# All fill-in places of the attention stage are numbered anew; the last step of a small transposed product stands further behind ScalarE's copy

## The chip, the core and the metric

The kernel runs on one core of a Trainium2 chip. A core has TensorE for matrix products and transposes (PE in the rows; its weight loads are PEld), VectorE (DVE), ScalarE (ACT), GpSimd (POOL), and SyncE (SP), whose queue issues most of the transfers. They read their instructions in program order and meet through semaphores. The metric is the time of one execution on the device, in microseconds (us).

## What the kernel computes

Three parts follow one another; `B, H, S, D = 4, 8, 768, 64`.

```
q_assign, k_assign = argmax of (normalised q, k) . (normalised centroids)      # 16 clusters per head
scores = scale * q @ k.T, and -1e9 where q_assign != k_assign
attn   = exp(scores - max(scores)) / (sum + 1e-9);   x = attn @ v              # x: 3072 x 512
h = x @ w_in;  g = h * cos(h);  y = g @ w_out                                   # 512 -> 2048 -> 512
logits = y @ phi;  dispatch = softmax over tokens;  combine = softmax over slots
out = combine @ (relu((dispatch.T @ y) @ w1) @ w2)                              # 8 experts, 4 slots each
```

## The kernel before

**The attention stage** covers the first half of the time and is the only part that the change touches. The 32 (batch, head) combinations are taken as 16 pairs of heads. For each pair `i` a *stack* `st` in on-chip memory (three of them, used in turn) holds q and k, each split in a high and a low part, and rows that carry the cluster mask and the row maximum. A score tile is the sum of two products with this stack (lines 446 and 447, `s<-st`), `score` has one tile of 128 keys by 384 queries for each head `h` and step `u` (12 steps a pair), and ScalarE turns each tile into exponentials (line 450, `a<-s`). So one pair is 12 steps of two score tiles, 48 products of line 446/447, and this loop over 16 x 12 steps `g` is written once:

```
for g in range(GE):
    for h in range(2):
        run_fill(g, h)
        score(i, ...)
    run_fill(g, 2); psum_add(i, u); run_fill(g, 3)
```

**Everything else of the stage is filled in between.** `run_fill(g, pos)` issues what has been put at position `pos` (0 to 3) of step `g`; positions 0 and 1 are ahead of the step's first and second score tile, 2 and 3 behind them. Tables of numbers set the places: a number `x` means step `g + x//4` from the pair's own start, position `x % 4`, and the fraction orders what shares a position. `FIRST` is for the first pair, `POS` for the 13 pairs in the middle, `NEXT` and `LAST` for the last two. What is placed:

- the next pair's stack: transposes of q and k (`T`: `prep_T`, `tpq`, `tpk`, line 268), the high and low parts (`prep_hi`, `prep_lo`), the cluster products, maxima and mask rows (`c`, `m`, `rows`), and copies within the stack, which are put off for some positions (`defer`) and then issued by SyncE (line 175)
- the row maxima: 24 products `sm` for each pair (line 400), each followed by a reduction on VectorE (line 402); `fin` gathers them, transposes them (`mrow`, line 415) and copies two rows into the stack through SyncE (`smax_row`)
- the value products `av` (line 459, `o<-a,vt`): 12 groups of 4; their order in the table decides how many stand side by side
- sums of the exponentials (`sumq`), sums of v (`prep_vm2`, `vm`)
- the conversion of 64-bit weights to 32 bits, two blocks a pair, in 8 steps `cv` on VectorE, ScalarE and GpSimd (`conv_do`), and the load `cl` of the next block
- for half of the blocks a small product with phi in three steps `wp`: four transposes `wt`, four products `wp` whose result ScalarE copies to `wq` (line 552), and a transpose of that, `wr` (line 556, `wphi_sum`), whose result VectorE sums

`prep_T` (from the third pair's stack on), `sm`, `mrow`, `cl`, `ct`, `eqt`, `mt`, `vm`, `sum`, `wt`, `wp` and `wr` share a ring of three banks of the product memory, taken in program order (`mbank`): a product waits until the bank of the third one before it has been read. Score tiles have three banks of their own, value products one.

In the first pair the mask rows of its own stack are written late: `rows0(1, 0, h, ACT)` (line 367), for the second half of the queries, whose places are `r0c`. The products `sm` of the first pair for queries of that half (`sm0`) and its later score tiles read them.

Of the kernel before, what the change touches and what calls it, by code (L numbers as in the profile page):

```python
# [26 lines left out]
def clustered_attention_then_soft_moe(  # L27
# [51 lines left out]
    vm = const.tile([P, NPAIR], F32, name="vm")  # L79
# [71 lines left out]
    with ExitStack() as a:  # L151
# [9 lines left out]
        T = {}  # L161
# [408 lines left out]
        def at4(g, q, f, *args):  # L570
# [1 line left out]
            at(g + x // 4, x % 4, f, *args, rank=q - x if q != x else 0.5)  # L572

        POS = {
            "T": [1.308, 13.876, 1.089, 5.872, 25.746, 36.055, 14.541, 35.775],
            "c": [16.843, 31.522],
            "m": [32.535, 32.994, 33.715, 36.49],
            "rows": [36.873, 43.945, 43.068, 42.752],
            "ld": 32.617,
            "cv": [[1.267, 6.08, 6.296, 16.916, 17.01, 17.372, 17.997, 18.854], [23.969, 30.541, 31.284, 32.698, 46.461, 46.996, 47.088, 47.142]],  # L580
            "wp": [22.636, 36.3, 36.578],
            "sm": [28.2, 31.753, 25.657, 7.038, 27.872, 18.018, 29.863, 4.585, 33.271, 20.202, 11.647, 6.495, 37.608, 42.706, 46.397, 45.847, 46.576, 24.17, 36.506, 9.889, 1.582, 37.875, 41.562, 38.508],
            "fin": [1.573, 5.263, 34.676, 37.539],
            "vm": [34.193, 45.742, 15.753],
            "cl": [2.501, 42.906],
            "av": [33.349, 33.353, 33.357, 33.361, 33.365, 33.369, 49.465, 49.469, 49.473, 49.477, 49.481, 49.485],
        }
        FIRST = {
            "T": [11.933, 13.351, 14.016, 14.265, 22.414, 33.022, 23.121, 40.828],
            "c": [20.876, 24.238],  # L590
            "m": [24.829, 25.602, 27.504, 31.599],
            "rows": [35.559, 41.933, 35.178, 47.346],
            "ld": 27.056,
            "hl1": [4.573, 11.085, 2.498, 12.153],
            "p1": [0.493, 6.362, 8.509, 9.612, 10.885, 13.533],
            "rows1": [20.017, 14.551, 20.333, 15.204],
            "one1": 12.589,
            "ld2": 3.852,
            "cl0": 22.601,
            "sm0": [0.73, 3.159, 0.429, 5.394, 1.277, 0.812, 14.931, 17.953, 16.508, 13.98, 15.389, 15.817, 16.123, 18.564, 11.559, 18.991, 9.813, 16.449],  # L600
            "fin0": [7.049, 9.9, 19.506, 19.912],
            "sm1": [33.923, 25.966, 23.596, 34.913, 28.869, 21.44, 22.363, 35.531, 30.988, 25.828, 21.408, 31.03, 31.941, 31.182, 37.18, 44.547, 46.392, 41.954, 41.697, 45.967, 47.974, 41.852, 45.504, 36.04],
            "fin1": [35.625, 40.713],
            "vm": [2.043, 5.623],
            "av": [15.327, 16.374, 19.171, 19.479, 22.394, 27.138, 31.368, 35.743, 35.838, 43.045, 46.406, 47.768],
            "r0c": [0.631, 0.302],
        }
        NEXT = {
            "cv": [[0.394, 0.437, 0.698, 2.152, 6.295, 7.495, 8.058, 19.811], [9.426, 12.828, 16.693, 17.691, 17.936, 20.568, 23.949, 35.345], [27.565, 29.065, 29.167, 30.486, 34.096, 36.446, 36.936, 41.49]],
            "wp": [19.895, 23.514, 35.069, 43.672, 45.817, 47.564],  # L610
            "sm": [21.695, 24.397, 11.934, 7.684, 27.445, 16.489, 17.35, 1.48, 1.969, 22.001, 24.625, 29.74, 13.73, 36.394, 19.994, 32.733, 41.217, 44.01, 39.92, 43.68, 45.934, 33.344, 5.07, 42.168],
            "fin": [0.258, 6.344, 30.741, 34.194],
            "vm": [6.804, 16.472, 23.722],
            "cl": [3.32, 18.679, 25.571],
            "av": [14.329, 14.502, 14.506, 14.551, 22.244, 22.964, 34.139, 34.149, 34.159, 43.43, 43.459, 57.281],
        }
        LAST = {
            "cv": [[1.943, 3.444, 3.447, 3.887, 3.892, 3.901, 4.34, 14.881], [11.025, 13.344, 14.301, 14.914, 17.834, 24.542, 29.982, 31.011], [33.835, 34.438, 38.539, 38.774, 42.047, 45.521, 46.04, 47.203]],
            "wp": [36.509, 39.65, 42.446],
            "fin": [1.822, 4.268],  # L620
            "vm": [5.423, 24.404, 26.852],
            "cl": [3.923, 23.538],
            "xp": [4.425, 5.64, 17.033],
            "av": [14.033, 14.043, 14.092, 14.388, 26.165, 26.175, 38.144, 38.279, 38.307, 38.559, 59.688, 61.83],
        }

        def place_conv(n, g, pl, x):
# [771 lines left out]
```

## Time and profile before

| | us |
|---|---|
| median of 3 runs | 879.15 |
| the runs | 878.90, 879.15, 2150.93 |
| the profiled execution | 879.05 |
| its span, first to last instruction | 877.2 |

| engine | busy us | share of the span | instructions |
|---|---|---|---|
| PE | 858.8 | 98% | 5978 |
| PEld | 617.9 | 70% | 5978 |
| DVE | 666.3 | 76% | 1391 |
| ACT | 628.4 | 72% | 1307 |
| POOL | 461.8 | 53% | 345 |

Busy time is the union of the instructions' spans on an engine; products overlap one another on PE, so its share says whether it had work, not how fast it went. The chain of work that ended last lies on PE for 93% of the span and on ACT for 3%. The attention stage ends at about 440 us; the MLP and the experts follow and use the engines in the same way before and after the change.

### The profile page before, as it was taken

To read this page: it belongs to the slowest core of one execution; us is meant where nothing else is said; L and a number is where in the kernel's file an instruction comes from. 1 tells how busy PE (TensorE), PEld (TensorE's weight loads), DVE (VectorE), ACT (ScalarE), POOL (GpSimd) and SP (SyncE) were. 2 spreads that over 40 slices of the span, in tenths; PEclk is the share of its full clock that TensorE was granted. 3 is DMA by queue.
4 is the path that set the end of the run, shared out by engine and by line. 5 is a ranking of instruction groups with operands and counts; after the bars stand their busy time and mean duration, and the time that the engine had idled before them with its cause. 6 is when DMAs were issued, how large, how long until landed. Compare 5 with 4: busy or idle time off the path is not lost.

```text
span 877.2 us, 16786 instructions
## 1 busy us (share of the span) xinstructions
PE 858.8 (98%) x5978; PEld 617.9 (70%) x5978; DVE 666.3 (76%) x1391; ACT 628.4 (72%) x1307; POOL 461.8 (53%) x345
## 2 busy tenths in 40 slices
PE   8999999999999999999999999999999999999995
PEld 4676767676777776776578877877787787777453
DVE  6798898988898988899877767776776777766203
ACT  6898888898888898886656775765666576577323
POOL 4578889888898888898953222222322222210000
PEclk9999999999999999999999999999999999999997
DMA  8766766656766656744323233321011010178998
GB/s 185 178 164 173 178 177 160 177 157 173 185 172 166 166 162 175 178 141 129 115 60 98 86 130 121 90 79 49 25 31 43 25 49 25 48 270 312 386 374 292
DMA packets 124742, 129.50 MB, mean 148 GB/s; under 512 B 57850, under 2 KB 101108, under 8 KB 124660
## 3 DMA queue, kind: packets, MB, share of 16 engines
q1 hardware_dynamic: 122948, 128.02, 50.2%
q8 instruction: 47, 0.77, 0.4%
q10 hardware_dynamic: 1712, 0.43, 0.3%
q14 instruction: 35, 0.29, 0.1%
HBM read 86.18 MB, written 16.97 MB: 118 GB/s over the span
## 4 chain that ended last, share of the span: by engine, by line
PE 93%; ACT 3%; DVE 1%; DMA 1%; issue 0%; ACTq 0%; DVEq 0%
PE h L139 30%; PE o L459 15%; PE sm L400 8%; PE s L446 8%; PE s L447 7%; PE gt L894 5%; PE lp L924 2%; PE accp L1007 2%; PE he L1240 2%; PE so L1269 2%; PE sum L484 1%; PE cl L308 1%; PE tpk L268 1%; PE tpq L268 1%; PE wt L542 1%; PE fo L1316 1%
## 5 line engine op out<-in xcount | busy, mean ns | idle before, releaser
L477 POOL TENSOR_TENSOR ps<-ps,a 128x768 f32<-128x768 f32 x124 | 229.9, 1854 | 37.5 <-ACT a L450 31.3
L139 PE MATMUL h<-wc,xhi 128*128 128x512 f32 x768 | 248.6, 404 | 0.0
L402 DVE TENSOR_REDUCE mc<-sm 128x1 f32<-128x384 f32 x384 | 195.9, 551 | 39.3 <-PE sm L400 38.3
L450 ACT ACTIVATE a<-s 128x384 f32<-128x384 f32 x384 | 174.0, 495 | 13.2 <-PE s L447 10.0
L139 PEld LDWEIGHTS h<-wc,xhi 128*128 128x128 f32 x768 | 137.1, 188 | 38.6 <-issue 11.7
L139 PE MATMUL h<-wc,xlo 128*128 128x512 f32 x384 | 153.0, 398 | 0.0
L446 PE MATMUL s<-st 96*128 96x384 f32 (+1 forms) x384 | 137.4, 358 | 0.0
L459 PE MATMUL o<-a,vt 128*64 128x384 f32 x768 | 133.8, 492 | 0.0
L447 PE MATMUL s<-st 128*128 128x384 f32 x384 | 130.4, 340 | 0.0
L400 PE MATMUL sm<-st 96*128 96x384 f32 x384 | 127.9, 367 | 0.1
L146 ACT ACTIVATE kk<-h 128x512 f32<-128x512 f32 x96 | 57.4, 598 | 76.8 <-DVE gg L887 33.1
L459 PEld LDWEIGHTS o<-a,vt 128*64 128x64 f32 x768 | 51.4, 136 | 62.4 <-issue 60.5
L106 POOL TENSOR_TENSOR xr<-xr 128x512 f32<-128x512 f32 x24 | 32.0, 1332 | 101.2 <-DMA xr<-recs 101.2
L400 PEld LDWEIGHTS sm<-st 96*128 96x128 f32 x384 | 71.7, 189 | 18.5 <-issue 7.0
L139 PEld LDWEIGHTS h<-wc,xlo 128*128 128x128 f32 x384 | 72.1, 188 | 16.9
L446 PEld LDWEIGHTS s<-st 96*128 96x128 f32 (+1 forms) x384 | 73.5, 191 | 12.9 <-issue 10.2
L147 DVE TENSOR_SCALAR kk<-kk 128x512 f32<-128x512 f32 x96 | 54.4, 567 | 34.3 <-ACT kk L146 34.2
L110 POOL TENSOR_TENSOR xr<-xr 128x512 f32<-128x512 f32 x24 | 31.8, 1327 | 90.3 <-DVE xr L108 90.3
L447 PEld LDWEIGHTS s<-st 128*128 128x128 f32 x384 | 72.6, 189 | 0.0
L148 DVE SCALAR_TENSOR_TENSOR kk<-kk,h 128x512 f32<-128x512 f32 x96 | 66.0, 688 | 3.3
L474 POOL TENSOR_TENSOR ps<-a,a 128x768 f32<-128x768 f32 x31 | 56.7, 1830 | 15.3 <-ACT a L450 15.3
L877 ACT ACTIVATE kk<-kk 128x512 f32<-128x512 f32 x96 | 60.1, 626 | 0.6 <-DVE kk L148 0.4
(242 smaller groups left out, 1414.0 us busy)
## 6 DMA issues: line engine op xcount, KB each, us to landing
st<-st SPq DMA_DIRECT2D x128, 192.0 KB
w<-in_moe_w_dram SPq DMA_DIRECT2D x8, 2048.0 KB
wh<-in_moe_w_dram SPq DMA_DIRECT2D x23, 512.0 KB
w<-in_moe_w_out_dram SPq DMA_DIRECT2D x16, 512.0 KB
w<-in_moe_w_in_dram SPq DMA_DIRECT2D x16, 512.0 KB
vt<-in_v_dram SPq DMA_DIRECT2D x16, 384.0 KB
xnum<-num SPq DMA_DIRECT2D x32, 192.0 KB
xr<-xnum SPq DMA_DIRECT2D x24, 256.0 KB
```

The costliest lines, as they stand in the source:

```text
L139: PE.matmul(h, lhsT=x[:, d, :], rhs=wc[f][:, w, d, :], start=(n == 0), stop=(n == 3 * DT - 1))
L146: ACT.activation(out=a, in_=h, func=AF.Copy, scale=1.0 / TWO_PI)
L148: DVE.scalar_tensor_tensor(out=a, in0=a, scalar=-TWO_PI, in1=h, op0=ALU.mult, op1=ALU.add)
L400: PE.matmul(m[:, 0:QW], lhsT=st[0:96, Q1 + h, qt * P:(qt + 1) * P], rhs=st[0:96, K1 + h, half * QW:(half + 1) * QW], start=True, stop=True)
L402: DVE.tensor_reduce(out=s["mc"][:, col:col + 1], in_=m[:, 0:QW], op=ALU.max, axis=AX.X)
L446: PE.matmul(x[:, 0:QW], lhsT=st[0:n, K1 + h, ks], rhs=st[0:n, Q1 + h, qs], start=True, stop=False)
L447: PE.matmul(x[:, 0:QW], lhsT=st[:, K2 + h, ks], rhs=st[:, Q2 + h, qs], start=False, stop=True)
L450: ACT.activation(out=T[i][u][:, h, :], in_=x[:, 0:QW], func=AF.Exp, scale=scale)
L459: PE.matmul(s["o"][64 * h:64 * h + 64, 0:QW], lhsT=s["v"][:, h, kt, :], rhs=t[:, h, :], start=(kt == 0), stop=(kt == KT - 1))
L474: (DVE if i == NPAIR - 1 and qc else POOL).tensor_tensor(out=ps, in0=s[u - 1], in1=t, op=ALU.add)
L477: (DVE if i == NPAIR - 1 and qc else POOL).tensor_tensor(out=ps, in0=ps, in1=t, op=ALU.add)
L877: ACT.activation(out=r, in_=r, func=AF.Sin, scale=0.5)
```

## The change

Every number of the four tables (lines 574 to 625) is another one; no other line differs. Each engine has as many instructions of each kind as before, and the loop with its score tiles stands as it did. A few rows of the tables, cut from the diff:

```diff
 POS = {
-    "wp": [22.636, 36.3, 36.578],
+    "wp": [24.809, 36.663, 41.156],
-    "fin": [1.573, 5.263, 34.676, 37.539],
+    "fin": [1.689, 5.264, 31.017, 37.302],
-    "vm": [34.193, 45.742, 15.753],
+    "vm": [23.652, 40.191, 15.215],
...
 FIRST = {
-    "sm0": [0.73, 3.159, 0.429, 5.394, 1.277, 0.812, 14.931, 17.953, 16.508, 13.98, ...],
+    "sm0": [0.422, 1.709, 0.83, 0.857, 3.191, 3.976, 17.629, 18.569, 17.326, 8.361, ...],
-    "r0c": [0.631, 0.302],
+    "r0c": [4.451, 8.347],
...
 NEXT = {
-    "av": [14.329, 14.502, 14.506, 14.551, 22.244, 22.964, 34.139, 34.149, 34.159, 43.43, 43.459, 57.281],
+    "av": [14.003, 14.013, 14.023, 14.521, 23.425, 23.435, 34.48, 34.904, 36.015, 43.053, 43.14, 51.341],
```

The tenth number of `sm0` is that of the product sm 15.

**PE, end of the pair 5 (as of each middle pair), before.** `sN_u_h` is a score tile of pair N, `sm6_n` a row-maximum product of the next pair, `mt` its mask product, `wp` and `wr` the last two steps of the small product; the number behind each name only counts.

```order
L446 MATMUL s5_8_1_2516<-st2_121 128x384
L447 MATMUL s5_8_1_2516<-st2_121 128x384
L550 MATMUL wp4_2532<-wt_4_2423,phis_79 32x128 x4
L349 LDWEIGHTS cum_135
L349 MATMUL mt7_2539<-eqT7_2514,cum_135 128x384
L400 MATMUL sm6_18_2543<-st0_119 128x384
L556 MATMUL wr4_2546<-ident_68,wq_4_2537 128x128
L446 MATMUL s5_9_0_2551<-st2_121 128x384
L447 MATMUL s5_9_0_2551<-st2_121 128x384
```

Between the products `wp`, whose result ScalarE copies, and `wr`, which reads the copy, stand a mask product and one `sm`; the transpose `mrow6_0` comes one score tile later.

**PE, the same place in the change**, from `wp` on; behind the last row of this piece follow the two products of a score tile, and then the rows of the next piece.

```order
L550 MATMUL wp4_2540<-wt_4_2449,phis_79 32x128 x4
L349 LDWEIGHTS cum_135
L349 MATMUL mt7_2547<-eqT7_2527,cum_135 128x384
L446 MATMUL s5_9_0_2551<-st2_121 128x384
L447 MATMUL s5_9_0_2551<-st2_121 128x384
L415 MATMUL mrow6_0_2556<-ident_68,m6_6_0_2495 6x128
L400 MATMUL sm6_22_2560<-st0_119 128x384
L446 MATMUL s5_9_1_2565<-st2_121 128x384
L447 MATMUL s5_9_1_2565<-st2_121 128x384
L383 MATMUL vm5_2573<-ident_68,vs5_2437 128x128
L400 MATMUL sm6_16_2576<-st0_119 128x384
```

The transpose `mrow` and the `vm` transpose now stand between `wp` and `wr`, each alone ahead of one `sm`.

```order
L446 MATMUL s5_10_0_2579<-st2_121 128x384
L447 MATMUL s5_10_0_2579<-st2_121 128x384
L556 MATMUL wr4_2584<-ident_68,wq_4_2545 128x128
L400 MATMUL sm6_15_2587<-st0_119 128x384
L446 MATMUL s5_10_1_2590<-st2_121 128x384
L447 MATMUL s5_10_1_2590<-st2_121 128x384
L400 MATMUL sm6_21_2596<-st0_119 128x384
L400 MATMUL sm6_23_2599<-st0_119 128x384
L400 MATMUL sm6_17_2609<-st0_119 128x384
L446 MATMUL s5_11_0_2612<-st2_121 128x384
L447 MATMUL s5_11_0_2612<-st2_121 128x384
L400 MATMUL sm6_13_2617<-st0_119 128x384
```

Seven products and transposes behind `mrow` take a bank of the ring before `sm6_17`: `sm6_22`, `vm5`, `sm6_16`, `wr4`, `sm6_15`, `sm6_21` and `sm6_23`. `sm6_17` takes the bank of `sm6_15`. On VectorE their reductions stand in the same order, with no other work between them.

**ACT, first pair, before**, from the copy of the first row of maxima on (`mrow0_0_0`); `mt0v` is the mask product of the first stack, `a0_u_h` an exponential.

```order
L438 ACTIVATE st0_119<-mrow0_0_0_318 1x384
L367 ACTIVATE st0_119<-mt0v_249,hsel_143 32x384
L310 ACTIVATE cs1_328<-cl1_329 128x384
L367 ACTIVATE st0_119<-mt0v_249,hsel_143 32x384
L450 ACTIVATE a0_0_345<-s0_0_0_342 128x384
L450 ACTIVATE a0_1_353<-s0_1_0_350 128x384
L282 ACTIVATE st1_120<-kT1_301 128x768
L282 ACTIVATE st1_120<-qT1_281 128x768
L450 ACTIVATE a0_2_375<-s0_2_0_372 128x384
L450 ACTIVATE a0_3_388<-s0_3_0_385 128x384
L450 ACTIVATE a0_4_403<-s0_4_0_400 128x384
```

**ACT, first pair, in the change.**

```order
L438 ACTIVATE st0_119<-mrow0_0_0_318 1x384
L282 ACTIVATE st1_120<-qT1_281 128x768
L310 ACTIVATE cs1_328<-cl1_329 128x384
L282 ACTIVATE st1_120<-kT1_301 128x768
L450 ACTIVATE a0_0_345<-s0_0_0_342 128x384
L450 ACTIVATE a0_1_353<-s0_1_0_350 128x384
L367 ACTIVATE st0_119<-mt0v_249,hsel_143 32x384
L450 ACTIVATE a0_2_375<-s0_2_0_372 128x384
L450 ACTIVATE a0_3_394<-s0_3_0_391 128x384
L367 ACTIVATE st0_119<-mt0v_249,hsel_143 32x384
L450 ACTIVATE a0_4_405<-s0_4_0_402 128x384
```

The second mask row (the second line 367) stood ahead of the exponentials; now it stands behind both parts of the next stack (line 282), four exponentials and the first mask row.

**PE, first pair, in the change**, around the product `sm0_15`, which reads that second mask row.

```order
L400 MATMUL sm0_7_365<-st0_119 128x384
L400 MATMUL sm0_11_368<-st0_119 128x384
L446 MATMUL s0_2_0_372<-st0_119 128x384
L447 MATMUL s0_2_0_372<-st0_119 128x384
L318 MATMUL ct1_377<-ident_68,cs1_328 128x128 x3
L446 MATMUL s0_3_0_391<-st0_119 128x384
L447 MATMUL s0_3_0_391<-st0_119 128x384
L400 MATMUL sm0_15_399<-st0_119 128x384
L446 MATMUL s0_4_0_402<-st0_119 128x384
L447 MATMUL s0_4_0_402<-st0_119 128x384
```

`sm0_15` stands right behind the tile `s0_3_0`, whose second product ran at 22.13 us before. 

**SyncE's queue, end of a pair, before.** `st1<-st1` are copies within a stack, the last of which read what an earlier copy wrote; `xnum` stores attention results, `mrow` rows are the two row-maximum copies that the next pair's first score tile needs.

```order
L175 DMA sums1_85<-sume4_2374 4x384
L175 DMA wod_92<-val_8_2267 128x512
L175 DMA st1_120<-st1_120 64x768 x2
L183 DMA qt8_2478<-in_q_dram 128x6x64 x2
L183 DMA kt8_2481<-in_k_dram 128x6x64 x2
L175 DMA xnum1_81<-num5_0_2508 128x384
L175 DMA st1_120<-st1_120 64x768 x2
L175 DMA st0_119<-mrow_6_0_2558 1x3x128 x2
L504 DMA w64_10_2595<-in_moe_w_out_dram 128x1024
```

**SyncE's queue, the same place in the change.**

```order
L175 DMA sums1_85<-sume4_2377 4x384
L175 DMA wod_92<-val_8_2256 128x512
L175 DMA st1_120<-st1_120 64x768 x7
L175 DMA xnum1_81<-num5_0_2520 128x384
L175 DMA st1_120<-st1_120 64x768
L175 DMA st0_119<-mrow_6_0_2558 1x3x128 x2
L504 DMA w64_10_2605<-in_moe_w_out_dram 128x1024
L504 DMA w64_11_2668<-in_moe_w_in_dram 128x1024
```

Seven copies within the stack now stand together ahead of the store, and an eighth behind it, right ahead of the `mrow` copies.

## Rows read from the trace of the kernel before

**Rows 1.** The page's head: span of the profiled execution
```profile
span 877.2 us, 16786 instructions
```

**Rows 2.** Stage view: stretch, busy time of each engine with instructions, clock, DMA
```profile
180.00:230.00 50.00, 49.91 (x328) 34.53 (x326) 44.00 (x86) 42.20 (x93) 43.12 (x32) 1.00 0.65 173
```

**Rows 3.** The product wr: durations (min/median/max, ns); who it waited for (us, times)
```profile
L556 PE MATMUL wr<-ident,wq x16: 270/329/329, 70.4 to 439.5; 128*128 128x128 f32 x16
...
  ACT wq L552: 4.6, 13
```

**Rows 4.** Timeline of PE around one wr: start us, us, engine, instruction
```profile
175.80 0.47 PE L400 MATMUL sm<-st 96*128 96x384 f32 x1
176.31 0.33 PE L556 MATMUL wr<-ident,wq 128*128 128x128 f32 x1
176.40 0.42 PE L446 MATMUL s<-st 96*128 96x384 f32 x1
176.66 0.34 PE L447 MATMUL s<-st 128*128 128x384 f32 x1
176.84 0.27 PE L415 MATMUL mrow<-ident,m 128*6 128x128 f32 x1
176.92 0.64 PE L400 MATMUL sm<-st 96*128 96x384 f32 x2
177.40 0.34 PE L446 MATMUL s<-st 96*128 96x384 f32 x1
...
180.39 0.34 PE L446 MATMUL s<-st 96*128 96x384 f32 x1
...
181.50 4.09 PE L459 MATMUL o<-a,vt 128*64 128x384 f32 x24
```

**Rows 5.** Timeline of PE: a row-maximum transpose that runs into three others
```profile
186.69 0.27 PE L415 MATMUL mrow<-ident,m 128*6 128x128 f32 x1
186.80 0.49 PE L268 MATMUL tpk<-ident,kt 128*128 128x128 f32 x3
```

**Rows 6.** Timeline of PE around a short run of value products
```profile
422.79 0.34 PE L447 MATMUL s<-st 128*128 128x384 f32 x1
423.06 0.87 PE L459 MATMUL o<-a,vt 128*64 128x384 f32 x4
423.85 0.44 PE L446 MATMUL s<-st 96*128 96x384 f32 x1
424.14 0.34 PE L447 MATMUL s<-st 128*128 128x384 f32 x1
```

**Rows 7.** Timeline of DVE at the end of a pair
```profile
177.15 0.28 DVE L417 TENSOR_SCALAR mrow<-mrow 6x128 fp32r<-6x128 f32 x1
177.40 2.42 DVE L402 TENSOR_REDUCE mc<-sm 128x1 f32<-128x384 f32 x5
179.73 0.28 DVE L384 TENSOR_REDUCE vm<-vm 128x1 f32<-128x128 f32 x1
```

**Rows 8.** Timeline of ACT in the first pair
```profile
19.16 0.57 ACT L367 ACTIVATE st<-mt0v,hsel 32x384 fp32r<-32x384 f32 x1
19.86 0.49 ACT L310 ACTIVATE cs<-cl 128x384 f32<-128x384 f32 x1
...
20.98 0.88 ACT L450 ACTIVATE a<-s 128x384 f32<-128x384 f32 x2
...
22.63 0.83 ACT L282 ACTIVATE st<-qT 128x768 fp32r<-128x768 f32 x1
```

**Rows 9.** Timeline of PE in the first pair
```profile
22.13 0.34 PE L447 MATMUL s<-st 128*128 128x384 f32 x1
...
24.64 0.44 PE L400 MATMUL sm<-st 96*128 96x384 f32 x1
```

**Rows 10.** Waits of SyncE's queue, 40 to 440 us: total, times, longest
```profile
SPq L175 <- DMA st<-st: 5.4, 4, 2.4
```

**Rows 11.** Timeline of SyncE's queue: two row-maximum copies
```profile
177.45 1.51 SPq L175 DMA_DIRECT2D st<-mrow  x2
```

More of the change, by code (lines that the diff above doesn't have):

```diff
@@ L574, in clustered_attention_then_soft_moe @@
         POS = {
[L575 to L580, printed above, removed]
-            "wp": [22.636, 36.3, 36.578],
-            "sm": [28.2, 31.753, 25.657, 7.038, 27.872, 18.018, 29.863, 4.585, 33.271, 20.202, 11.647, 6.495, 37.608, 42.706, 46.397, 45.847, 46.576, 24.17, 36.506, 9.889, 1.582, 37.875, 41.562, 38.508],
@@ L583, in clustered_attention_then_soft_moe @@
-            "fin": [1.573, 5.263, 34.676, 37.539],
-            "vm": [34.193, 45.742, 15.753],
-            "cl": [2.501, 42.906],
-            "av": [33.349, 33.353, 33.357, 33.361, 33.365, 33.369, 49.465, 49.469, 49.473, 49.477, 49.481, 49.485],
+            "T": [1.31, 1.34, 9.77, 10.839, 26.266, 29.286, 16.149, 24.271],
+            "c": [15.765, 27.704],
+            "m": [28.746, 29.874, 33.865, 36.95],
+            "rows": [37.833, 42.374, 44.441, 44.954],
+            "ld": 15.236,
+            "cv": [[0.41, 1.005, 8.709, 9.354, 11.469, 12.21, 14.059, 15.763], [27.776, 28.508, 29.63, 31.497, 33.764, 35.123, 45.912, 46.22]],
@@ new lines, in clustered_attention_then_soft_moe @@
+            "wp": [24.809, 36.663, 41.156],
+            "sm": [11.851, 16.362, 29.148, 15.957, 1.846, 17.033, 22.515, 5.359, 27.098, 7.167, 6.376, 4.099, 35.124, 45.752, 46.069, 41.248, 40.921, 44.998, 21.373, 31.808, 20.412, 42.877, 37.456, 42.894],
+            "fin": [1.689, 5.264, 31.017, 37.302],
+            "vm": [23.652, 40.191, 15.215],
+            "cl": [1.751, 44.843],
+            "av": [33.166, 33.17, 33.174, 33.178, 33.182, 33.186, 49.485, 49.489, 49.493, 49.497, 49.501, 49.505],
@@ L587, in clustered_attention_then_soft_moe @@
         }
         FIRST = {
[L589 to L604, printed above, removed]
@@ L605, in clustered_attention_then_soft_moe @@
-            "av": [15.327, 16.374, 19.171, 19.479, 22.394, 27.138, 31.368, 35.743, 35.838, 43.045, 46.406, 47.768],
-            "r0c": [0.631, 0.302],
+            "T": [12.667, 12.961, 15.588, 16.806, 20.822, 30.347, 22.108, 40.024],
+            "c": [20.086, 21.126],
+            "m": [21.713, 22.463, 23.221, 32.107],
+            "rows": [34.994, 46.829, 37.665, 41.52],
+            "ld": 30.916,
+            "hl1": [0.285, 12.323, 0.669, 12.739],
+            "p1": [0.446, 5.584, 5.605, 6.266, 11.115, 13.963],
@@ new lines, in clustered_attention_then_soft_moe @@
+            "rows1": [17.292, 18.048, 17.5, 18.817],
+            "one1": 14.724,
+            "ld2": 2.191,
+            "cl0": 18.144,
+            "sm0": [0.422, 1.709, 0.83, 0.857, 3.191, 3.976, 17.629, 18.569, 17.326, 8.361, 17.223, 16.515, 13.026, 18.123, 17.791, 17.284, 18.138, 18.401],
+            "fin0": [5.782, 10.22, 18.679, 18.985],
+            "sm1": [20.735, 22.697, 24.299, 27.247, 29.838, 33.473, 30.005, 34.03, 23.639, 22.577, 26.418, 34.994, 42.942, 20.431, 45.605, 41.743, 42.355, 37.973, 39.417, 44.884, 38.695, 42.275, 46.147, 46.224],
@@ L607, in clustered_attention_then_soft_moe @@
+            "fin1": [37.794, 39.061],
+            "vm": [5.781, 18.292],
+            "av": [17.435, 18.273, 18.709, 18.733, 22.71, 23.186, 31.527, 38.749, 42.378, 42.472, 46.845, 47.418],
+            "r0c": [4.451, 8.347],
         }
         NEXT = {
-            "cv": [[0.394, 0.437, 0.698, 2.152, 6.295, 7.495, 8.058, 19.811], [9.426, 12.828, 16.693, 17.691, 17.936, 20.568, 23.949, 35.345], [27.565, 29.065, 29.167, 30.486, 34.096, 36.446, 36.936, 41.49]],
-            "wp": [19.895, 23.514, 35.069, 43.672, 45.817, 47.564],
@@ L611, in clustered_attention_then_soft_moe @@
[L611 to L614, printed above, removed]
-            "av": [14.329, 14.502, 14.506, 14.551, 22.244, 22.964, 34.139, 34.149, 34.159, 43.43, 43.459, 57.281],
+            "cv": [[0.162, 0.262, 0.97, 1.922, 7.97, 9.726, 11.671, 15.399], [12.751, 13.395, 15.935, 16.455, 19.048, 21.746, 24.619, 31.558], [30.532, 33.857, 34.979, 35.984, 39.594, 39.742, 40.043, 41.06]],
@@ new lines, in clustered_attention_then_soft_moe @@
+            "wp": [16.888, 24.599, 33.362, 43.288, 45.087, 47.511],
+            "sm": [29.789, 25.024, 15.245, 30.695, 17.315, 22.97, 7.165, 19.295, 13.365, 25.467, 5.966, 33.422, 3.399, 43.708, 41.329, 12.35, 20.486, 36.366, 45.597, 47.042, 1.497, 44.136, 14.837, 41.311],
+            "fin": [0.055, 1.495, 34.963, 37.206],
+            "vm": [21.847, 42.961, 24.943],
+            "cl": [3.824, 18.694, 34.432],
+            "av": [14.003, 14.013, 14.023, 14.521, 23.425, 23.435, 34.48, 34.904, 36.015, 43.053, 43.14, 51.341],
@@ L616, in clustered_attention_then_soft_moe @@
         }
         LAST = {
[L618 to L624, printed above, removed]
+            "cv": [[0.067, 0.19, 0.628, 4.123, 4.195, 5.423, 7.81, 15.226], [8.354, 9.711, 9.733, 10.335, 10.829, 12.675, 16.809, 22.67], [22.887, 33.352, 38.019, 38.498, 40.15, 41.441, 41.54, 45.813]],
@@ L625, in clustered_attention_then_soft_moe @@
+            "wp": [33.129, 39.031, 45.03],
+            "fin": [0.001, 9.466],
+            "vm": [1.082, 32.521, 23.859],
+            "cl": [4.163, 9.652],
+            "xp": [4.169, 10.662, 17.698],
+            "av": [14.056, 14.066, 14.076, 22.163, 22.173, 22.198, 38.068, 38.078, 38.088, 38.098, 48.388, 51.257],
         }
```

## The prediction

> **What bounds the kernel now.** I read the page's head first, then a stage view, then the order of the work around one pair's end, in that order because the change moves work only within the attention stage. The profiled execution took 879.05 us, of which the span is 877.2 [rows 1]; the median of the runs is 879.15, a tenth above, so sums are made against 879.05 and stand for the median as well. In the middle of the stage PE is busy for 49.91 of 50.00 us at a granted clock of 1.00, that is at 2.4 GHz, while DVE has 44.00, ACT 42.20 and POOL 43.12 [rows 2]. So PE sets the time, and the reader is to see in the timeline how: products of 384 columns start 0.18 us apart although each lasts 0.34 (176.66 to 176.84 is one such step) [rows 4]. PE is filled by the starts of its instructions. As each engine keeps the same instructions, the sum is made of three kinds of things only: waits of PE that go, waits that come, and steps between unlike instructions that cost more than 0.18.
>
> How much such a step costs is in the same rows. Around the lone transpose `mrow`, from the product ahead of it to the score product behind two `sm`, 0.74 us pass (176.66 to 177.40) where three products alone would take 0.54: a lone transpose costs 0.20 [rows 4]. One that runs into other transposes costs 0.11 (186.69 to 186.80) [rows 5]. A run of 24 value products takes 4.09, so 0.17 each [rows 4]; four of them between score products take 1.35 (422.79 to 424.14), of which 4 x 0.17 are theirs and 2 x 0.18 the steps between three score products, so entering and leaving a run of value products costs 0.31 [rows 6].
>
> **Part 1: the wait of `wr` goes.** In 13 of its 16 occurrences `wr` waited for ScalarE's copy `wq`, 4.6 us in all [rows 3]; those 13 are the middle pairs. By starts: from the `sm` at 175.80 to `wr` at 176.31 0.51 us pass [rows 4], where the two `sm` behind `mrow` took 0.24 each (176.92 to 177.40). So 0.27 a pair is wait, the rest of the 0.35 that the view counts is the change of kind. Now a score tile, `mrow`, `sm`, a second tile, `vm`, `sm` and a third tile stand between `wp` and `wr`: at least 1.6 us, against the some 0.5 that the copy needs after its wait by the same gap. The wait is gone: 13 x 0.27 = **-3.5**. The other transpose of maxima, of the second half of the queries, ran into three others [rows 5] and now stands alone between products, for 0.20 instead of 0.11: 13 x 0.09 = **+1.2**.
>
> **Part 2: a new wait for a bank at the pair's end.** After `mrow` the new order of PE is `sm22`, tile, `vm`, `sm16`, tile, `wr`, `sm15`, tile, `sm21`, `sm23`, `sm17`. Taken from `mrow`'s start, `sm17` is reached after 11 products at 0.18 and 3 lone transposes at 0.20, at 2.58 us. It takes the bank of `sm15`, which VectorE must have reduced. VectorE takes the row scaling first, 0.31 after the transpose's start (176.84 to 177.15) and has `sm22` from 0.56 on (177.40) [rows 4, 7]; then 0.48 for each reduction (2.42 for 5) and 0.28 for `vm` [rows 7]; for `wr`, with as many columns as `vm`, I take the same 0.28. So `sm22` ends at 1.04, `vm` at 1.32, `sm16` at 1.80, `wr` at 2.08, `sm15` at 2.56. A semaphore takes another 0.04 (`mrow` on PE ends at 177.11, VectorE starts at 177.15) [rows 4, 7]: 2.60 against 2.58, a tie within what the steps are known to. I take a wait of 0.08 a pair, 13 x 0.08 = **+1.0**. Bounds: 0, if VectorE is a little earlier, and a whole reduction, 13 x 0.48 = 6.3, if something else stands ahead of it there. The tie is the nearer, because no other VectorE work is placed in this piece.
>
> **Part 3: the first pair.** `sm0_15` reads the second mask row, which ScalarE now writes behind eight other instructions. From 19.16, where ScalarE took up its first mask row before [rows 8], they are two parts of the next stack at 0.83, `cs` at 0.49, four exponentials at 0.44, the first mask row at 0.57 and itself at 0.57: 1.66 + 0.49 + 1.76 + 1.14 = 5.05, so 24.21. PE reaches `sm0_15` one step behind the tile `s0_3_0`, whose second product started at 22.13 [rows 9], with what stands differently ahead of it at about 22.4. The wait would be 1.8 at most, and PE, standing still, lets ScalarE, VectorE and the transfers get ahead, so that later waits of the first pair shrink (as that of the `sm` at 24.64, which took 0.44 instead of 0.34 [rows 9]). Between 0 and 1.8 I take the middle, **+0.9**.
>
> **Part 4: the last but one pair** has 7 runs of value products instead of 6 (+0.31) and 5 lone transposes instead of 3 (of 0.09 more than in a run each): **+0.4** together with the rounding of the rest. The other moves cost nothing: conversion steps, loads and stack copies lie on DVE, ACT, POOL and SP, each with 6 us or more in 50 to spare [rows 2]. If VectorE's cover were gone, the conversion steps would show as the case "VectorE late" below.
>
> Sum: -3.5 + 1.2 + 1.0 + 0.9 + 0.4 = 0.0, so **879.0 us**.
>
> The Trainium skill speaks for a larger gain than this sum: "Perfetto Trace Analysis", in its section on identifying the most-contended engine, says that the busy share of products does not tell how close TensorE is to its limit, and that the share of weight loads does. By that rule the 34.53 us of weight loads in 50 [rows 2] would leave room in every pair. It is the rival "room in PE".
>
> **The rivals.**
>
> *Slower, through SyncE's queue.* The two `mrow` copies, which the next pair's first score product needs, are issued at the pair's end, at 177.45, taking 1.51 us until 178.96, and that product starts at 180.39 [rows 4, 11]: a slack of 1.43. In the new order seven copies within the stack stand ahead of the store of results, and an eighth, which reads what an earlier copy wrote, right ahead of the `mrow` copies. SyncE stopped for such a landing 4 times before, for 5.4 us in all and up to 2.4 [rows 10]. If the eighth copy waits for its predecessor after the `mrow` rows are ready, everything behind it waits, and PE with it: a wait of 2.4 beyond the slack costs 1.0 a pair, and all of 2.4 if the slack is gone, 13 x 1.0 to 2.4 = 13 to 31, so 892 to 910. The point from which it decides is a landing later than about 1.4 us behind the row scaling. Against it: the seven copies are issued long before `mrow`, and the store between them gives them time. For it: the waits are real, and the queue is in order. A weaker form gives 883 to 892. The Trainium skill, "DMA: Bandwidth & Descriptors", in its section on the anatomy of one DMA, states the same: transfer engines do not wait on semaphores, the wait is on the issuing sequencer ahead of dispatch; the SyncE waits of [rows 10] agree with it. I give 0.08 to this rival, 0.03 of it beyond 2%.
>
> *VectorE late.* A conversion step or a reduction more ahead of `sm15` makes part 2's wait 0.48 a pair: 6.3 instead of 1.0, 884.3. VectorE has 6 us in 50 to spare, but not everywhere. 0.06.
>
> *No new waits.* Part 2's tie falls the other way and the first pair absorbs the late row: 879.05 - 3.5 + 1.2 + 0.4 = 877.2, or 876 to 877.5. 0.12.
>
> *The edit does nothing for `wr`.* If `wr` still waits, for instance for its bank instead of the copy, the -3.5 is missing: 882.5. Against it: the bank it takes is that of `sm22`, read at 1.04 by part 2, where PE reaches `wr` at about 1.5 (six products and two lone transposes). 0.02.
>
> *Room in PE.* If PE's steps were not set by its starts, a better order could take more than 2% off, below 861.5. Starts of 0.18 at a product's 0.34 speak against it [rows 4]. 0.01.
>
> **How the numbers follow.** The sum's own case has 0.71 and 877.5 to 881.5, by bounds of parts 2 and 3. The range reaches to "no new waits" below, with half a microsecond for steps that I did not cost, and to "VectorE late" above: 875.5 to 884.5. Outside lie most of the SyncE rival and "room in PE", and what I overlooked, under 2 in 10. A difference under 2%, 861.5 to 896.6, counts as no change here. Faster by more has 0.01, for room in PE, slower by more 0.03, for the SyncE queue, and within 0.96.
>
> **What would show it.** In the profile after: `wr` no longer waits for `wq`, and starts at most 0.2 us behind the product ahead of it (part 1). `sm17` starts 0.25 to 0.3 us behind `sm23` instead of 0.18, put down to a reduction (part 2). In the first pair, `sm0_15` waits for ScalarE's line 367 by up to 1.8 us (part 3). SyncE's waits for stack copies stay near 5.4 us in all; were they ten times that, with PE idle at each pair's start, the first rival is right. A pair's length that differs by more than 0.3 us from before, in either direction, would make the prediction wrong.

## The result, and the profile after

The changed kernel takes 890.25 us (median of 4 runs, 889.69 to 890.61), the kernel before 879.59 in the runs beside it: a ratio of 1.0122, 95% interval 1.0110 to 1.0134. It is slower by 11 us, where 879.0 was forecast and the range ended at 884.5. (The 2150.93 among the runs of before is a disturbed run and counts in no comparison.) The profiled execution took 890.50 us.

The page of the changed kernel, its head, busy times and the chain that ended last:

```profile
span 888.7 us, 16805 instructions
...
PE 863.8 (97%) x5978; PEld 616.2 (69%) x5978; DVE 678.2 (76%) x1391; ACT 633.2 (71%) x1307; POOL 464.3 (52%) x345
...
PE 84%; DVE 7%; ACT 3%; DMA 2%; issue 2%; POOL 1%; SPq 0%; DVEq 0%; ACTq 0%; POOLq 0%
```

Two things differ: DVE is busy for 678.2 us instead of 666.3 with the same 1391 instructions, and it holds 7% of the chain instead of 1%. Some VectorE instruction has become longer, and PE waits behind it. The stage view of the changed kernel (columns as in [rows 2]) agrees: PE stands for 0.77 us in 50 instead of 0.09, at the same granted clock.

```profile
180.00:230.00 50.00, 49.23 (x320) 35.34 (x318) 43.62 (x86) 45.01 (x97) 42.42 (x27) 1.00 0.59 163
```

The timeline of PE in the changed kernel, from the start of one middle pair to the start of the next:

```profile
185.64 0.34 PE L446 MATMUL s<-st 96*128 96x384 f32 x1
...
200.44 0.34 PE L400 MATMUL sm<-st 96*128 96x384 f32 x1
...
201.65 0.34 PE L447 MATMUL s<-st 128*128 128x384 f32 x1
202.37 0.44 PE L400 MATMUL sm<-st 96*128 96x384 f32 x1 [0.38 <-DVE mc L402]
...
212.67 0.34 PE L446 MATMUL s<-st 96*128 96x384 f32 x1
```

The pair takes 27.03 us. Before it took 26.46, from 180.39 [rows 4] to this product of the kernel before:

```profile
206.85 0.33 PE L446 MATMUL s<-st 96*128 96x384 f32 x1
```

The product at 202.37 is sm19. It starts 0.72 behind the one ahead of it instead of 0.18, so 0.54 are lost, and it waits for the bank of the sm at 200.44, called sm8. Why that one's reduction was late stands one instruction further up, on VectorE and on GpSimd of the changed kernel:

```profile
197.64 2.41 DVE L402 TENSOR_REDUCE mc<-sm 128x1 f32<-128x384 f32 x5
199.96 1.89 DVE L298 TENSOR_TENSOR st<-kT,st 128x768 fp32r<-128x768 f32 x1
201.77 0.54 DVE L402 TENSOR_REDUCE mc<-sm 128x1 f32<-128x384 f32 x1
```

```profile
199.21 1.83 POOL L477 TENSOR_TENSOR ps<-ps,a 128x768 f32<-128x768 f32 x1
```

Line 298 is the subtraction that makes the low part of k (`prep_lo`). It stands while GpSimd is in a running sum of 768 columns. All its instructions (durations min/median/max in ns), first in the kernel before, then in the changed one:

```profile
L298 DVE TENSOR_TENSOR st<-kT,st x15: 935/960/1187, 25.8 to 385.3; 128x768 fp32r<-128x768 f32 x15
```

```profile
L298 DVE TENSOR_TENSOR st<-kT,st x15: 939/1886/2019, 26.1 to 389.2; 128x768 fp32r<-128x768 f32 x15
```

So the same instruction takes twice as long. No row calls this a wait: the time is counted as VectorE being busy.

The kernel before had a smaller case of the same. Line 294, the subtraction for q, ran into a GpSimd addition of 128 columns there (line 378, 200.06 to 201.11) and ended 0.82 behind it, at 201.93. It went from 1.21 to 0.95 with the change, again first before, then after:

```profile
L294 DVE TENSOR_TENSOR st<-qT,st x15: 948/1207/1212, 24.5 to 386.2; 128x768 fp32r<-128x768 f32 x15
```

```profile
L294 DVE TENSOR_TENSOR st<-qT,st x15: 946/949/2408, 25.3 to 393.9; 128x768 fp32r<-128x768 f32 x15
```

Where the span's 11.5 us went, from the starts of the pairs' first score products in both traces:

| part | before us | after us | difference |
|---|---|---|---|
| up to the first pair | 20.16 | 20.37 | +0.2 |
| first pair | 31.97 | 34.11 | +2.1 |
| 13 middle pairs | 340.18 | 347.56 | +7.4 |
| last but one pair | 28.57 | 28.96 | +0.4 |
| last pair | 19.48 | 19.44 | 0.0 |
| MLP to the end | 436.83 | 438.31 | +1.5 |

### The profile page after: what moved, and what is told of

Same layout as the page of the kernel before. It is cut to its first block, busy times and chain, and to the rows that moved or that the text cites. A ratio compares the mean times of both kernels' runs of the same rounds, so it can differ in the third digit from the quotient of the medians.

```text
span 888.7 us, 16805 instructions
## 1 busy us (share of the span) xinstructions
PE 863.8 (97%) x5978; PEld 616.2 (69%) x5978; DVE 678.2 (76%) x1391; ACT 633.2 (71%) x1307; POOL 464.3 (52%) x345
## 4 chain that ended last, share of the span: by engine, by line
PE 84%; DVE 7%; ACT 3%; DMA 2%; issue 2%; POOL 1%; SPq 0%; DVEq 0%; ACTq 0%; POOLq 0%
PE h L139 28%; PE o L459 15%; PE sm L400 7%; PE s L446 6%; PE s L447 5%; PE gt L894 4%; DVE mc L402 4%; PE lp L924 2%; PE accp L1007 2%; DMA vt<-in_v_dram 2%; PE he L1240 2%; PE so L1269 2%; PE tpq L268 1%; PE sum L484 1%; PE cl L308 1%
## 5 line engine op out<-in xcount | busy, mean ns | idle before, releaser
L477 POOL TENSOR_TENSOR ps<-ps,a 128x768 f32<-128x768 f32 x124 | 236.9, 1910 | 23.6 <-ACT a L450 14.0
L450 ACT ACTIVATE a<-s 128x384 f32<-128x384 f32 x384 | 176.0, 495 | 8.3 <-PE s L447 4.1
L400 PE MATMUL sm<-st 96*128 96x384 f32 x384 | 134.3, 375 | 7.4 <-DVE mc L402 5.9
```

The lines of the kernel that those rows point to most:

```text
L400: PE.matmul(m[:, 0:QW], lhsT=st[0:96, Q1 + h, qt * P:(qt + 1) * P], rhs=st[0:96, K1 + h, half * QW:(half + 1) * QW], start=True, stop=True)
L450: ACT.activation(out=T[i][u][:, h, :], in_=x[:, 0:QW], func=AF.Exp, scale=scale)
L477: (DVE if i == NPAIR - 1 and qc else POOL).tensor_tensor(out=ps, in0=ps, in1=t, op=ALU.add)
```

## The experiments

**Theory (collision).** A VectorE instruction that reads two on-chip tensors cannot start beside a GpSimd instruction that does the same and waits until it has ended; the change moved line 298 into a GpSimd sum, and sm19 pays for it. **Rivals:** VectorE simply has too much in a row there; or the two engines share throughput.

### GpSimd's sums taken away at that place

```diff
-                psum_add(i, u)
+            elif not (1 <= i <= NPAIR - 3 and u in (4, 5)):
+                psum_add(i, u)
```

> The changed kernel, but in the 13 middle pairs GpSimd leaves out two of the twelve sums of exponentials, those of steps 4 and 5, so that it is idle when VectorE subtracts the high part of k (line 298); the sums come out short. Theory (collision): line 298 took 0.96 us before and 1.89 in the changed kernel because it waits for GpSimd's running sum, and the product sm19 behind it waits 0.54 a pair. Then line 298 falls to about 0.95, the gap ahead of sm19 falls from 0.72 to 0.18, a pair is 0.54 shorter and the kernel takes 890.3 - 7.0 = 883.3. Rival (VectorE has too much work in a row there whatever GpSimd does): line 298 stays near 1.9, the wait stays, 889 to 890.

Measured: 897.70, slower still, so the time was missed by 14 us. But line 298 fell to a median of 0.95 and sm19 to its 0.18. What came instead stands on VectorE and GpSimd of this kernel:

```profile
206.24 2.50 DVE L294 TENSOR_TENSOR st<-qT,st 128x768 fp32r<-128x768 f32 x1
```

```profile
206.10 1.81 POOL L474 TENSOR_TENSOR ps<-a,a 128x768 f32<-128x768 f32 x1 [1.12 <-ACT a L450]
```

With VectorE on time, the next subtraction (q, line 294, 0.95 in the changed kernel) met the beginning of the next sum, and PE waited later on, in this kernel's timeline:

```profile
183.50 0.34 PE L447 MATMUL s<-st 128*128 128x384 f32 x1
184.58 0.27 PE L415 MATMUL mrow<-ident,m 128*6 128x128 f32 x1 [0.74 <-DVE mc L402]
```

The collision moved, it did not go. So both had to be taken away together:

```diff
-                psum_add(i, u)
+            elif not (1 <= i <= NPAIR - 3 and u in (4, 5, 7, 8)):
+                psum_add(i, u)
+            elif u == 8:
+                ...
+                POOL.tensor_tensor(out=T[i]["ps", 1], in0=T[i][7], in1=T[i][8], op=ALU.add)
```

> The changed kernel, in the 13 middle pairs without GpSimd's sums of steps 4 and 5, and with the second half's first sum (steps 6 and 7) replaced by one that waits for step 8: GpSimd is idle at both subtractions of VectorE, line 298 (k) and line 294 (q). The sums come out short. Theory (collision): both take 0.95 us, the wait ahead of sm19 (0.54) goes and no wait at mrow takes its place as it did when only the sums of 4 and 5 were out; a pair takes 27.03 - 0.54 = 26.49, the kernel 890.3 - 7.0 = 883.3. Rival (VectorE's order is too tight anyhow, another wait appears): 888 to 898.

Measured: 880.25. Both subtractions are back at one length, by line in this kernel:

```profile
L298 DVE TENSOR_TENSOR st<-kT,st x15: 936/960/1072, 25.7 to 380.6; 128x768 fp32r<-128x768 f32 x15
...
L294 DVE TENSOR_TENSOR st<-qT,st x15: 946/949/2410, 24.8 to 384.2; 128x768 fp32r<-128x768 f32 x15
```

A middle pair takes 26.35, that is 0.68 less than with the change and 0.11 less than before. GpSimd makes three sums fewer a pair here, so this does not show that the new order is the better one. (The one 2.41 is in the first pair, where no sum was taken out.)

### All work kept, the collision made smaller

Two kernels keep every operation; both have FIRST of before, which alone gives 887.77 (below).

```diff
 POS = {
-            "T": [1.31, 1.34, 9.77, 10.839, 26.266, 29.286, 16.149, 24.271],
+            "T": [1.31, 1.34, 9.77, 10.839, 26.266, 29.286, 16.149, 20.6],
```

> The changed kernel with FIRST of before (887.8 by itself) and the subtraction of line 298 earlier in POS (24.271 to 20.6), where by the trace GpSimd ends one sum and begins the next. Theory (collision): line 298 takes between 0.95 and 1.4 us, the wait ahead of sm19 (0.54 a pair) goes; the reductions of sm18 and sm6 come later, so ct may wait up to 0.4: 881 to 886. Rival (wherever it stands it meets a sum): 1.9 again and 887 to 889.

Measured: 885.48. Line 298 has a median of 0.97, sm19 waits no more, a pair takes 26.8. The price is where it was expected, behind the subtraction, in the timeline of PE:

```profile
197.87 0.34 PE L447 MATMUL s<-st 128*128 128x384 f32 x1
198.13 0.44 PE L400 MATMUL sm<-st 96*128 96x384 f32 x1
198.60 0.55 PE L318 MATMUL ct<-ident,cs 128*128 128x128 f32 x3
```

0.26 and 0.47 stand where 0.18 each would do: 0.37 of the 0.54 are given back.

```diff
-                (DVE if i == NPAIR - 1 and qc else POOL).tensor_tensor(out=ps, in0=ps, in1=t, op=ALU.add)
+                for h in range(2) if 1 <= i <= NPAIR - 3 else [slice(0, 2)]:
+                    (DVE if ...).tensor_tensor(out=ps[:, h], in0=ps[:, h], in1=t[:, h], op=ALU.add)
```

> The changed kernel with FIRST of before (887.8 by itself), where GpSimd makes each running sum of the middle pairs in two halves of 384 columns instead of one of 768 (line 477), all work kept. Theory (collision, VectorE waits until GpSimd's instruction has ended): a half takes about 1.0 us instead of 1.84 (128 columns 0.46, 512 columns 1.28, 768 columns 1.84 in the trace), so line 298 waits at most 1.0 instead of 1.84; it takes 0.95 to 1.5 instead of 1.9, the wait ahead of sm19 is 0.2 or less, a pair 26.5 to 26.7: 881 to 884, if GpSimd's some 2 us more a pair stay covered. Rival (VectorE and GpSimd share throughput over the whole overlap, however it is cut): line 298 stays at 1.9, 888.

Measured: 880.33, that is 7.4 less than 887.77 with every sum made and nothing moved. By line in this kernel:

```profile
L298 DVE TENSOR_TENSOR st<-kT,st x15: 936/1240/1381, 25.7 to 380.1; 128x768 fp32r<-128x768 f32 x15
```

With GpSimd's instructions cut in two, the subtraction waits for a shorter one. The pair takes 26.43; the wait of sm19 is gone, and the 0.24 a pair of sm17 (part 2 below) is still there. This is the clearest of the runs: only the length of what is collided with was changed. One such meeting in this kernel, on GpSimd and on VectorE:

```profile
194.58 1.00 POOL L478 TENSOR_TENSOR ps<-ps,a 128x384 f32<-128x384 f32 x1
```

```profile
195.17 1.24 DVE L298 TENSOR_TENSOR st<-kT,st 128x768 fp32r<-128x768 f32 x1
```

The subtraction ends 0.83 behind the end of the half sum (196.41 and 195.58). In the changed kernel it ends 0.81 behind the whole sum (201.85 and 201.04), and with the sums of steps 4 and 5 left out line 294 ends 0.83 behind (208.74 and 207.91). So its end follows the end of GpSimd's instruction, whenever it began itself, and that instruction keeps its own length (1.00, 1.83, 1.81). That speaks against shared throughput and for a wait for the whole instruction.

This kernel does not beat the one before (ratio 1.0012, 1.0003 to 1.0022).

```diff
-            at4(g, t[7], prep_lo, j, "k")
+            at4(g, t[7], prep_lo, j, "k", POOL if g else DVE)
```

> The changed kernel with the subtraction of line 298 done on GpSimd instead of VectorE in the middle pairs, same place in the order. Theory (collision): VectorE gets 1.89 us a pair back ahead of sm8's reduction, the wait of 0.54 ahead of sm19 goes: 883.3, if GpSimd's 1.85 more a pair (42 of 50 busy before) lies beside the rest. Rival (GpSimd becomes late): its sums hold up the exponentials' buffers and with them the score tiles, 888 or more.

Measured: 966.63. The rival named for this run was right, and far underpriced: GpSimd became the late one. The granted clock of TensorE fell as well, to between 0.87 and 0.93 in stretches of 50 us from 50 to 450 us, where PE was busy for 41 to 47 of 50; the change had 1.00, the 2.4 GHz level, and 49.23 (180 to 230 us). So the loss is waits and slower products together, and no run here parts them. PE's waits in the middle pairs of this kernel (us in total, times, longest):

```profile
PE s L446 <- ACT a L450: 25.5, 11, 2.6
PE s L446 <- DMA st<-mrow: 14.2, 11, 2.4
```

### The bank at the pair's end, and `wr`

```diff
 POS = {
-    "sm": [..., 44.998, 21.373, ...],
+    "sm": [..., 47.5, 21.373, ...],
```

> The changed kernel with sm17 of the middle pairs moved from behind sm21 and sm23 to the pair's last position (44.998 to 47.5). Theory (bank): the three sm in a row took 0.78 instead of 0.54, 0.24 a pair, because sm17's bank was not yet reduced; moved, it comes 0.9 us later on PE and finds the bank free: 13 x 0.2 = 2.6 less, 887.7. Rival (VectorE's row of reductions is late as a whole): the next sm waits instead, 890.3.

Measured: 895.31, slower by 5. In the row where sm17 had stood, a score tile now came 0.32 behind the last sm instead of 0.18, and a transpose of the next pair waited; PE's waits in the middle pairs:

```profile
PE tpq L268 <- DVE mc L402: 3.9, 12, 0.3
PE sm L400 <- DVE mc L402: 3.3, 13, 0.3
```

The first line is the new one. The second is the wait of sm19 from the changed kernel, a little shorter. The rival (VectorE is late in the whole row) held, with more than it asked, though it was a transpose that waited and not an sm.

In the kernel before, `wr` alone:

```diff
-            "wp": [22.636, 36.3, 36.578],
+            "wp": [22.636, 36.3, 41.156],
```

> The kernel before with one number changed: wr of the middle pairs at 41.156, as in the change. Theory: 13 waits of 0.27 go, 879.6 - 3.5 = 876.1. Rival: wr now stands in the row of reductions that VectorE has at the pair's end and takes a bank there, so a sm waits instead for up to one short reduction (0.28): 876 to 879.8.

Measured: 879.39, ratio 1.0007 (0.9998 to 1.0016): no gain. The wait for ScalarE's copy `wq` became one for ScalarE's copy of the mask, by the waits of the weight loads in this kernel:

```profile
PEld sm L400 <- ACT z L351: 3.9, 13, 0.3
```

In the ring of three banks the third product behind the mask product `mt` takes its bank. Without `wr` in between, that third one is reached sooner, and ScalarE's copy of the mask, which follows `wq` at once, isn't done.

```diff
-            "wp": [22.636, 36.3, 36.578],
+            "wp": [22.636, 36.3, 37.55],
```

> The kernel before with one number changed: wr of the middle pairs directly behind the transpose mrow (36.578 to 37.55). With wr late at 41.156 its wait of 0.27 came back as waits of mrow and the next sm for banks, since wr no longer stood between mt and them in the ring of three; behind mrow it keeps the bank of sm12 as it was, and two transposes stand side by side. Theory (bank ring): 13 x 0.2 to 0.3 less, 875 to 876.5. Rival (the copy's time has to be paid somewhere on PE in any case): 879 again.

Measured: 879.16, ratio 1.0000 (0.9991 to 1.0008). Now `wr` itself waits for the mask's copy, 3.9 us in 13 times. The rival held. A third try kept both waits away by moving two sm as well:

```diff
-            "wp": [22.636, 36.3, 36.578],
+            "wp": [22.636, 36.3, 45.7425],
-            "sm": [..., 24.17, 36.506, 9.889, 1.582, 37.875, ...],
+            "sm": [..., 24.17, 36.2, 9.889, 1.582, 38.4, ...],
```

> The kernel before with three numbers of POS changed: wr behind the transpose vm (45.7425), sm18 ahead of wp (36.2), sm21 one score tile later (38.4). wr late alone gained nothing because the third product behind mt (its bank in the ring of three) then waited for ScalarE's copy of the mask; here that third product is sm21, over 1 us behind mt. Theory (bank ring): neither wait is left, 13 x 0.25 = 3.3 less, 875.8. Rival (the row of reductions on VectorE then holds up a later sm): 878 to 880.

Measured: 886.96. Neither of the two theories of this run: both waits are gone, and PE ran into ScalarE's exponentials, 13 times in the middle pairs, and from the `wr` at 181.84 to the sm behind it another 0.35 passed:

```profile
PE s L446 <- ACT a L450: 4.9, 13, 0.4
```

### The tables, one at a time

> The kernel before with the changed table POS alone, the other tables as before. Theory: the 13 middle pairs carry 0.55 each, 7.1 of the 11.2: 879.2 + 7.1 = 886.3, and up to 1.2 more if the long issue of a transfer behind the attention stage (2.13 instead of 0.61 us) comes with this table. Rival (the first pair's part grows into the middle pairs): clearly less than 5.

POS of the change in the kernel before: 892.18. The middle pairs take 27.04 each in the median, as with the whole change, so they carry their 7 us alone. The rest is a seam: the last but one pair took 33.9, with a wait of 2.7 for mask rows (line 360); NEXT of before presumably doesn't fit this POS.

> The changed kernel with the table FIRST of before. Theory: the first pair loses its two waits (1.5 for the mask row ahead of sm15, 1.1 for VectorE behind a subtraction of 2.41 us): 34.11 goes back to about 32.0, so 890.3 - 2.1 = 888.2. Rival: the waits come from the stack's transfers and stay, 890.

FIRST of before in the changed kernel: 887.77. The first pair is back at 31.99, and its two waits are gone. In the changed kernel they were these, on PE:

```profile
22.64 0.34 PE L447 MATMUL s<-st 128*128 128x384 f32 x1
24.33 0.45 PE L400 MATMUL sm<-st 96*128 96x384 f32 x1 [1.35 <-ACT st L367]
...
45.08 0.33 PE L447 MATMUL s<-st 128*128 128x384 f32 x1
46.35 0.44 PE L400 MATMUL sm<-st 96*128 96x384 f32 x1 [0.94 <-DVE mc L402]
```

The second lies behind another collision, a subtraction of 2.41 us at 43.42 beside a GpSimd sum that began at 43.18.

### Behind the attention stage

```diff
+        def more(i):
+            SP.dma_start(out=extra[i], in_=phi[0:P, 4 * i:4 * i + 4])
+
+        for i in range(4):
+            at(40 + 2 * i, 2, more, i)
```

> The changed kernel with four more loads of 2 KB by SyncE in the attention stage, which nothing reads. Theory (SyncE's own program code): the second transfer of the reciprocals behind the attention stage took 2.13 us to issue instead of 0.61 because a piece of SyncE's program was being loaded just then; four more instructions shift where the piece ends, the issue takes 0.6, the MLP's start loses its wait of 0.6 to 1.2: 889.3. Rival (that transfer waits for others, whatever the code): 1.4 to 2.1 again.

Measured: 889.87 in 2 runs, no change, and the transfer's issue is long again (two issues, together 2.34). SyncE's queue there, first before, then with the change:

```profile
455.16 1.26 SPq L100 DMA_DIRECT2D xr<-recs  x2
```

```profile
465.24 2.77 SPq L100 DMA_DIRECT2D xr<-recs  x2
```

The theory isn't supported; why the issue is longer stays open. Of the span's last 1.5 us, 1.3 were lost between 23 and 47 us behind the MLP's first product, after this issue, and 0.8 in the kernel with the loads. That the issue holds them up is likely by this order, but not shown.

## Why the prediction was wrong

**The step that failed** is the sentence near the end of part 4: the other moves "cost nothing", since VectorE, GpSimd and the others each have 6 us or more in 50 to spare [rows 2]. That row is an average of busy time. Line 298 was moved from a place where GpSimd ran short instructions of 128 columns to one where it ran a sum of 768, and its length rose from 0.96 to 1.89. A moved instruction was priced by its old row, as if it lasted as long anywhere. The 0.54 a pair that follow are 7.0 us, about what the middle pairs lost (7.4); parts 1 and 2 below nearly cancel there. The rival "VectorE late" had their size (0.48 a pair, 884.3) and was given 0.06; it named a longer queue as the cause, not a longer instruction.

The Trainium skill has the mechanism, on the page "SBUF — State Buffer", section "SBUF: two separate sides": VectorE and GpSimd share a pair of ports, taken as a lock for a whole instruction, by a VectorE operation with two inputs in this memory against a GpSimd operation that reads it; whoever starts first keeps it. The runs agree: 1.89 beside a sum of 768 columns, 1.24 beside halves, 0.95 with those sums out of its way. By that rule the place of every two-input VectorE instruction against GpSimd's would have had to be read from the order, which the prediction did not do. The trace of before had a sign of it, the 1.21 of line 294.

**Part 1** (-3.5 and +1.2). `wr` does wait no more, as forecast; in the changed kernel its row (before in [rows 3]) is this, and nothing stands under it as waited for:

```profile
L556 PE MATMUL wr<-ident,wq x16: 270/271/273, 74.9 to 449.9; 128*128 128x128 f32 x16
```

The -3.5 fits the account of the middle pairs: 7.0 for sm19, 3.1 for sm17 (part 2) and -3.5 make 6.6 of the 7.4; the other 0.8 is not taken apart. But the gain was not `wr`'s alone to give: by itself in the kernel before, the move gave a ratio of 1.0007, since the next ring product waited for ScalarE's next copy. The +1.2 for `mrow` alone was mis-sized. In the changed kernel, on PE:

```profile
182.32 0.34 PE L447 MATMUL s<-st 128*128 128x384 f32 x1
182.50 0.27 PE L383 MATMUL vm<-ident,vs 128*128 128x128 f32 x1
182.53 0.42 PE L400 MATMUL sm<-st 96*128 96x384 f32 x1
182.79 0.34 PE L446 MATMUL s<-st 96*128 96x384 f32 x1
```

From 182.32 to 182.79 are 0.47, 0.11 more than two steps of 0.18. A lone transpose costs 0.11, not 0.20, as much as one that runs into others [rows 5], so the term is 0. The 0.74 in [rows 4] held another 0.09, perhaps a wait; no row names it.

**Part 2** (+1.0). Right in place and mechanism, wrong in size: the three sm at the pair's end took 0.78 instead of 0.54, 0.24 a pair or 3.1 in all, against a forecast 0.08. PE came sooner than worked out, because each of three transposes was priced 0.09 too high. The rows for it:

```profile
183.80 0.94 PE L400 MATMUL sm<-st 96*128 96x384 f32 x3
184.58 0.34 PE L446 MATMUL s<-st 96*128 96x384 f32 x1
```

**Part 3** (+0.9). `sm15` waited 1.5 by its start (22.64 to 24.33, less 0.18), near the upper bound of 1.8; the 1.1 behind the second collision was in no term. Together the first pair lost 2.1.

**Part 4**, the last but one pair: +0.4 forecast, +0.39 measured. The number is partly luck: its terms make 0.31 + 2 x 0.09 = 0.49, and the 0.09 is the surplus of a lone transpose that was just found to be nothing.

**The slower rival, SyncE's queue**, did not come about: its waits for stack copies are 5.5 us in 4 times, longest 3.1, where before it was [rows 10]. Neither did "room in PE": with all work kept, the shortest usual middle pair of any run is the 26.43 of the halved sums, against 26.46 before.

## What to carry to other kernels

Where VectorE and GpSimd both run instructions with two on-chip inputs, look in the order for which of them meet after a move, and price a meeting at up to a whole instruction of the other engine; cutting the longer one in two is a cheap remedy. A lock shows as a longer instruction, not as a wait: compare one line's min, median and max between two kernels before looking at the waits. And where three engines are all near full, a wait that is removed from one copy tends to return at the next: price a removed wait by what is second latest, not by its own length.

## What the runs showed that was not expected

Taking work from GpSimd made the kernel 7.4 us slower (897.70 against 890.25), because it set VectorE's next subtraction 0.14 us behind the start of another sum, which made the subtraction 2.50 us long instead of 0.95. And the subtraction on GpSimd itself, 1.85 us in 27, cost 76 us, with the lower clock that came with it.
